# Attention and a gated feed-forward block: where eight blocks of probabilities are transposed

## The chip, the cores and the metric

The kernel runs on one core of a Trainium2 chip. The metric is the device time of one execution in microseconds (us). A core has five engines that run their own instruction lists in order and wait for each other by semaphores: TensorE (PE in the profile, with PEld for its weight loads), VectorE (DVE), ScalarE (ACT), GpSimd (POOL) and SyncE (SP), which here issues the DMA transfers.

## The reference

Sliding-window attention over 8 batches of 576 positions (8 heads of 64), whose output is the input of a gated feed-forward block on 4608 tokens.

```python
scores = scale * np.matmul(q, k.transpose(0, 1, 3, 2))
rel = pos[:, None] - pos[None, :]
mask = (rel >= 0) & (rel < window)          # window = 64
scores = np.where(mask, scores, -1000000000.0)
scores = scores - np.max(scores, axis=-1, keepdims=True)
attn = np.exp(scores)
attn = attn / (np.sum(attn, axis=-1, keepdims=True) + 1e-09)
out = np.matmul(attn, v)
...
x = np.ascontiguousarray(attn_out.transpose(0, 2, 1, 3)).reshape(B * S, H * D)
gate = 1.0 / (1.0 + np.exp(-(x @ w_gate)))
val = x @ w_val
return gate * val @ w_out
```

## The kernel before, in words

**Tiles and pairs.** The 4608 tokens are 12 tiles of 384; two tiles are a pair. The first pair goes through the feed-forward block by plain matrix products. The other five pairs (`s` = 1 to 5; the text calls `s` = 2 the second pair and `s` = 3 the third) use seven block products for each step of the 2 x 2 block scheme. Every number is held as a high and a low part, so that a product is three matmuls (line 641).

**Ups and downs.** The ups of a pair have 42 steps: 6 values of `k` by 7 products, and in each step one product for the gate half (`m` = 0) and one for the value half (`m` = 1), six matmuls each. Three PSUM banks per half are used again for all seven products; ScalarE copies the first product out (line 656), VectorE adds the others (lines 651 and 680), ScalarE makes the gate (`g`, line 424) and VectorE multiplies gate and value (`h<-g,...`, line 429). The downs have 42 steps as well, each with three matmuls for either output half (`y_0`, `y_1`), in the same six banks. Their right-hand sides are split parts of the hidden values: ScalarE writes the high part (line 723), VectorE the low one (line 724).

**Attention beside it.** A unit is one tile by one pair of heads. The attention of the pairs to come runs inside the ups, in visits. A visit (`stage_v`) at up 5, 12, 19, 26 or 33 forms the outputs of the last two units (line 380) and the scores of two new ones (line 225); VectorE adds the mask and takes the minimum (line 250), ScalarE the exponentials with their sums (line 258), VectorE inverts the sums (lines 265 and 266), GpSimd multiplies by them (line 275). Then the probabilities have to be transposed, half by half (two heads, two halves, `h`). There are two ways:

- `stage_b`: three matmuls with the identity on TensorE (line 329) and a copy by ScalarE (line 334) per half.
- `stage_d` and `stage_e`: ScalarE copies the 32-bit words into two planes of 16 bits (`pl`, line 347), a DMA transposes the planes (`plT`, line 350), and ScalarE joins them again (line 357).

In the visits of new units of the same next pair the first unit goes by planes and the second by TensorE. In the last visit of the second and third pair's ups, at up 33, the two units belong to the pair after the next, and both go by TensorE.

**What sets the order.** Every step is put on a list with a time of the plan's own clock, and the list is sorted; buffers rotate in the order of that list. A scheduler then lays each engine's instructions out in an order that keeps these dependences. The planes `pl` come from a ring of three buffers (`w32`), and so do `t1` tiles that prepare the next pair's input: `x_prep` forms, for either of two column blocks, the differences `t` and `xf` (lines 595 and 596). The transposed planes lie in buffers of the pool `xp` which the plan knows to be free. q and k of a unit have two buffers each (`q` and `k`), filled by loads on SP.

Of the kernel before, what the change touches and what calls it, by code (L numbers as in the profile page):

```python
# [14 lines left out]
U16 = mybir.dt.uint16  # L15
# [4 lines left out]
P = 128  # L20
# [3 lines left out]
UP = UT // 2  # L24
# [3 lines left out]
def attn_ffn(ctx: ExitStack, tc: tile.TileContext, qT, kT, vN, w_gate, w_val, w_out, out, outT):  # L28
# [9 lines left out]
    NP = DM // P  # L38
# [12 lines left out]
    xp = ctx.enter_context(tc.tile_pool(name="xp", bufs=1))  # L51
    mp = ctx.enter_context(tc.tile_pool(name="mp", bufs=2))
    ap = ctx.enter_context(tc.tile_pool(name="ap", bufs=1))
# [113 lines left out]
    xs, xf = {}, {}  # L167
# [169 lines left out]
                marks["pT"][NP * t + p] = cp.ins  # L337
            st[(t, p, h)] = pT

    def stage_d(t, p):  # L340


        free = [unit(t // 2, i) for i in (6, 7)]
        for h in range(2):
            halves = st[(t, p, h)].rearrange("p u c -> p (u c)").bitcast(U16).rearrange("p (n e) -> p e n", e=2)
            pl = mp.tile([P, 2, TT], U16, name=f"pl{h}_{t}_{p}", tag="w32", bufs=W32)
            nc.scalar.copy(pl, halves)
            ft, fp = free[h]
            plT = xp.tile([P, 2 * UP, P], U16, name=f"plT{h}_{t}_{p}", tag=f"xf{4 * (ft % 2) + fp}")
            nc.sync.dma_start_transpose(out=plT, in_=pl.rearrange("p e n -> p (e n)"))  # L350
            turned_of[(t, p, h)] = plT

# [410 lines left out]
    def put(tm, o, f, *a):  # L763
        events.append((tm, o, f, a))

    AHEAD = 2
    DPT = DNT / TB
    APT = (0.9, 0.8, 0.9, 1.5, 0, 2.7, 0, 0)
    stages = (stage_a, stage_b, stage_c, stage_s, stage_n, stage_v, stage_d, stage_e)
    LOAD_AHEAD = 8  # L770
    BEFORE, BEHIND = 0, 12
# [9 lines left out]
    for n in range(2 * NP):  # L781
        t, p = divmod(n, NP)
# [6 lines left out]
    def unit(s, n):  # L789
        return 2 * s + n // 2 % 2, n // 4 + n % 2 * 2  # L790
# [11 lines left out]
    for n, (x, y, z) in enumerate(((4.5, 7.5, 8.5), (9, 12, 13), (13.5, 16, 17), (17.5, 20.5, 22), (22.5, 25, 26), (26.5, 30, 31), (31.5, 35, 36), (36.5, 40, 41))):  # L802
        u = unit(1, n)
# [5 lines left out]
    def attend(i):  # L809
        nonlocal now  # L810
        for f, t, p, *done in fill.get(i, ()):
            if f == 5:
                for a in t or ():
                    put(now - LOAD_AHEAD, 8, load_qk, *a)
                    put(now + 2.8, 8.5, load_v, *a)
            if f in (0, 3):
                ahead = LOAD_AHEAD + (1.5 if t // 2 == 2 else 0)
                put(now - ahead, 8, load_qk, t, p)
                put(now - ahead, 8.5, load_v, t, p)
            put(now, 6, stages[f], t, p, *done)  # L820
            now += APT[f]
# [60 lines left out]
    for s in range(1, NS):  # L882
        fill.clear()

        def visit(key, *what):
            fill.setdefault(key, []).append(what)

        if s + 1 < NS:
            done = [unit(s + 1, i) for i in range(2)] if s > 2 else None
            for v, u in enumerate(DOUBLE):  # L890
                if s == 1 or done and v == 0:
                    continue
                new = [unit(s + 1, 2 * v + i) for i in range(2)] if v < NP else None
                if v == NP and s + 2 < NS:
                    new = [unit(s + 2, i) for i in range(2)]
                visit(("u", u), 5, new, done)
                for i, (a, tn, tb) in enumerate(zip(new[::-1] if new else (), (1.5, 2.5), (3.5, 5))):
                    visit(("u", u + tn), 4, *a)
                    if i == 0 and v < NP:
                        visit(("u", u + 2.5), 6, *a)  # L900
                        visit(("u", u + 6.5), 7, *a)
                    else:
                        visit(("u", u + tb), 1, *a)
                done = new
        if s == 1:
            visit(("u", 1), 1, *unit(s + 1, 0))
            for v, u in enumerate(VISITS, 1):
                visit(("u", u), 3, *unit(s + 1, v), unit(s + 1, v - 1), u % NPR)
                visit(("u", u + 1), 4, *unit(s + 1, v))
                visit(("u", u + 3.5), 1, *unit(s + 1, v))  # L910
            visit(("u", 41), 2, *unit(s + 1, 7))
        for k in range(NK):
            if s == 1:
                for m in range(2):
                    make = (-28 + 7 * m, -29 + 6 * m)[k] if k < 2 else -25 + 8 * m
                    put(now + make - 6, 7, sums_load, m, k)
                    put(now + make, 7, sums_make, m, k)
                    for i, at_cut in zip((0, 2), (-14 + 2 * m, -10 + 2 * m) if k == 0 else (-13 + 1.5 * m, -5 + 1.5 * m)):
                        put(now + at_cut, 7, sums_split, m, k, i)
                        put(now + at_cut + 4, 7, sums_store, m, k, i)  # L920
                for n, d in ((0, -23 if k == 0 else -14), (4, -12 if k == 0 else -4), (5, -9 if k == 0 else -1)):
                    put(now + d, 7.5, w_load, s, k, n)
            else:
                for n in range(NPR):
                    put(now - 22 + 2.1 * n, 7.5, w_load, s, k, n)
            for n in range(NPR):
                for m in range(2):
                    put(now, 9, product, s, k, n, m)
                    now += PRT
                    if m == 0:  # L930
                        attend(("u", NPR * k + n - 0.5))
                attend(("u", NPR * k + n))
            put(now + 0.5, 5, h_prep, s, k)
            if k < EXTRA:
                put(now + 3, 5.1, h_early, s, k)
        t0, at_down = now, []

        def x_parts(prep, free):
            for c in range(2):
                put(prep + 0.5 + c, 5, x_prep, s + 1, c)  # L940
                for n in range(NPR):
                    put(free(2 * n + c), 5.5, x_part, s + 1, n, c)
                    put(free(2 * n + c) + 0.9, 5.6, x_rest, s + 1, n, c)

        for n in range(NPR):
            if s == NS - 1 and n == NPR - 1:
                for q in range(2):
                    for k in range(NK):
                        if q == 0:
                            at_down.append(now)  # L950
                        put(now, 9, last_product, s, n, k, (q,))
                        now += PRT / 2
                continue
            for k in range(NK):
                at_down.append(now)
                put(now, 9, last_product, s, n, k)
                now += PRT
                attend(("d", NK * n + k))
        for i, tm in enumerate(at_down):
            if i < EXTRA + 2 * NPR:  # L960
                when = max(t0 - 14.5 + 2.1 * ((i - EXTRA) // 2 + 1), t0 - 5.2 if GUARD[0] <= i < GUARD[1] else t0 - 15, {5: t0 + 0.8, 11: t0 + 0.9, 17: t0 + 1}.get(i, t0 - 20))
            else:
                when = at_down[i - 19] + 1.2
            if i >= EXTRA:
                put(when, 5.2, h_part, s, *divmod(i, NK))
            if i % 2 == 0:
                put(at_down[i - 13] + 1.1 if i > 13 else t0 - 80 + 4 * i if s > 1 else t0 - 18 + 2 * i, 8.2, wo_load, s, i // 2)
        if s + 1 < NS:
            x_parts(at_down[20], lambda x: at_down[24 + x] + 1.3)
# [76 lines left out]
```

## Time and profile before

| | us |
|---|---|
| median of 3 runs | 940.41 |
| lowest, highest | 939.93, 940.72 |
| the profiled execution | 941.92 |
| span of its records | 940.1 |
| TensorE busy in the span | 924.1 |
| VectorE busy | 714.2 |
| ScalarE busy | 524.1 |

The granted clock of TensorE was full in every slice. A row in order of time gives its start, its length (from the first to the last end where it groups several), the engine, the line, the operation, the tiles and, in brackets, how long the engine was idle ahead of it and what ended that. Lengths overlap a little: on VectorE one 128x384 row is 0.55 us long, and the next starts 0.47 us after it.

### The profile page before, as it was taken

The numbers are of one execution on the slowest core, as the hardware profiler recorded it, in microseconds if no ns is written. First come the engines' busy times: TensorE is split into PE (matmuls) and PEld (weight loads), VectorE is DVE, ScalarE is ACT, GpSimd is POOL, SyncE is SP. The second block draws the span as 40 slices with busy tenths as digits, with TensorE's granted clock in tenths as the row PEclk, the third lists the DMA queues.
The fourth block names the chain that finished last, engine by engine and source line by source line (L and its number), as shares of the span: only waits on it lengthen the run. The fifth ranks groups of instructions, "written<-read, shape, count | busy, mean of one in ns | idle before, by whom it ended". The sixth has DMA issues, their size and how long they took to land.

```text
span 940.1 us, 20226 instructions
## 1 busy us (share of the span) xinstructions
PE 924.1 (98%) x7104; PEld 889.5 (95%) x7104; DVE 714.2 (76%) x1919; ACT 524.1 (56%) x1394; POOL 152.4 (16%) x232
## 2 busy tenths in 40 slices
PE   6999999999999999999999999999999999999998
PEld 4799999879999999999999999999999999999998
DVE  7999989788878975666985667796566896566882
ACT  7867677556566642766753276664156665222460
POOL 4211104703773000221100012100011100000000
PEclk9999999999999999999999999999999999999999
DMA  9899988979999989999889899989899788988475
GB/s 339 309 391 374 353 312 284 342 283 353 396 322 303 409 295 307 302 312 305 275 254 312 263 309 319 291 245 281 294 299 309 224 249 276 290 256 252 134 216 166
DMA packets 121510, 277.39 MB, mean 295 GB/s; under 512 B 27456, under 2 KB 49600, under 8 KB 121408
## 3 DMA queue, kind: packets, MB, share of 16 engines
q1 hardware_dynamic: 121408, 276.09, 89.1%
q8 instruction: 57, 0.93, 0.4%
q14 instruction: 45, 0.37, 0.1%
HBM read 220.20 MB, written 51.90 MB: 289 GB/s over the span
## 4 chain that ended last, share of the span: by engine, by line
PE 88%; DVE 5%; DMA 3%; ACT 2%; issue 1%; SPq 0%; POOL 0%; DVEq 0%; ACTq 0%; POOLq 0%
PE pr L641 45%; PE y L641 23%; PE ph L416 7%; PE y L464 3%; PE pr L380 2%; PE pp L329 2%; PE s L225 1%; ACT p L258 1%; DVE p L250 1%; PE pr L225 1%; PE s L380 1%; DMA a<-w32d 1%; DVE w L160 1%; DMA plT<-pl 1%; DMA q<-in_qT_dram 1%
## 5 line engine op out<-in xcount | busy, mean ns | idle before, releaser
L641 PE MATMUL pr<-x_T,wt 128*128 128x384 f32 x1224 | 221.7, 334 | 0.0
L641 PE MATMUL y<-h,wot 128*128 128x384 f32 x1260 | 219.9, 334 | 0.0
L641 PEld LDWEIGHTS y<-h,wot 128*128 128x128 f32 x1260 | 218.3, 188 | 0.7 <-DVE h L429 0.6
L641 PEld LDWEIGHTS pr<-x_T,wt 128*128 128x128 f32 x1224 | 212.8, 188 | 0.3 <-issue 0.3
L641 PE MATMUL pr<-x_B,wt 128*128 128x384 f32 x1008 | 188.4, 337 | 0.0
L641 PEld LDWEIGHTS pr<-x_B,wt 128*128 128x128 f32 x1008 | 174.4, 188 | 2.4 <-issue 1.9
L275 POOL TENSOR_TENSOR p<-p,rs 128x384 f32<-128x384 f32 x76 | 70.6, 942 | 515.6 <-DVE rs L266 240.0
L723 ACT CAST h<-h 128x384 fp32r<-128x384 f32 x210 | 104.3, 514 | 86.7 <-PE y L641 41.0
L724 DVE TENSOR_TENSOR h<-h,h 128x384 fp32r<-128x384 f32 x210 | 112.0, 562 | 23.2 <-ACT h L723 21.3
L258 ACT ACTIVATE p<-p,mn 128x128 f32<-128x128 f32 x288 | 110.9, 393 | 18.0 <-DVE mn L250 17.5
L416 PE MATMUL ph<-x,w 128*128 128x384 f32 x576 | 106.0, 338 | 0.9 <-DVE h L429 0.8
L416 PEld LDWEIGHTS ph<-x,w 128*128 128x128 f32 x576 | 99.7, 188 | 3.7 <-DVE h L429 1.3
L424 ACT ACTIVATE g<-c 128x384 f32<-128x384 f32 x90 | 47.0, 522 | 86.3 <-DVE c L680 80.1
L651 DVE TENSOR_TENSOR c<-pr,p 128x384 f32<-128x384 f32 x60 | 33.1, 551 | 36.3 <-PE pr L641 36.2
L429 DVE SCALAR_TENSOR_TENSOR h<-g,c 128x384 f32<-128x384 f32 x90 | 52.5, 583 | 8.0 <-ACT g L424 2.3
L258 ACT ACTIVATION_READ_ACCUMULATOR p<-p,mn 128x1 f32 x264 | 49.9, 189 | 0.0
L656 ACT COPY p<-pr 128x384 f32<-128x384 f32 x60 | 28.3, 474 | 36.6 <-PE pr L641 36.5
L651 DVE TENSOR_TENSOR u<-pr,p 128x384 f32<-128x384 f32 x60 | 33.0, 552 | 17.3 <-PE pr L641 17.3
L357 ACT COPY p<-plT 128x768 uint16<-128x768 uint16 x20 | 18.5, 926 | 40.7 <-DMA plT<-pl 40.7
L641 PE MATMUL pr<-x_T,ws 128*128 128x384 f32 x216 | 40.5, 339 | 0.0
L641 PEld LDWEIGHTS pr<-x_T,ws 128*128 128x128 f32 x216 | 37.2, 188 | 0.9 <-issue 0.3
L680 DVE TENSOR_TENSOR c<-pr,p 128x384 f32<-128x384 f32 x60 | 32.8, 554 | 5.3 <-PE pr L641 5.1
(188 smaller groups left out, 1246.2 us busy)
## 6 DMA issues: line engine op xcount, KB each, us to landing
wt<-wd SPq DMA_DIRECT2D x186, 512.0 KB, 4.6
wot<-wod SPq DMA_DIRECT2D x105, 512.0 KB, 4.7
v<-in_vN_dram SPq DMA_DIRECT2D x48, 384.0 KB, 5.7
wd<-ws SPq DMA_DIRECT2D x48, 256.0 KB, 5.5
k<-in_kT_dram SPq DMA_DIRECT2D x48, 224.0 KB, 5.6
q<-in_qT_dram SPq DMA_DIRECT2D x48, 192.0 KB, 5.6
w32d<-w SPq DMA_DIRECT2D x36, 256.0 KB, 5.1
wd<-w SPq DMA_DIRECT2D x36, 256.0 KB, 5.5
```

The lines of the kernel that those rows point to most:

```text
L258: exp = nc.scalar.activation(pt[:, u, :], pt[:, u, :], AF.Exp, bias=mn[:, u:u + 1], scale=-1.0, **sums)
L275: eng.tensor_mul(out=pt, in0=pt, in1=rs.unsqueeze(2).broadcast_to([P, UP, P]))
L380: pe(nc.tensor.matmul(oo[U // 2][h * BLK:(h + 1) * BLK, U % 2 * BLK:(U % 2 + 1) * BLK], vt[:, U, h * BLK:(h + 1) * BLK], pT[h][:, U // 2, ...
L416: pe(nc.tensor.matmul(ph, l, r, start=i == 0, stop=i == len(prs) - 1))
L424: act = nc.scalar.activation(g, c, AF.Tanh)
L429: nc.vector.scalar_tensor_tensor(out=out, in0=g, scalar=1.0, in1=val, op0=ALU.add, op1=ALU.mult)
L641: pe(nc.tensor.matmul(ps, l, r, start=first and i == 0, stop=last and i == 2, skip_group_check=not check))
L651: marks["plus"] = nc.vector.tensor_add(out=o, in0=ps, in1=a).ins
L656: nc.scalar.copy(st["p1"], ps)
L680: nc.vector.tensor_add(out=c, in0=in0, in1=in1)
L723: nc.scalar.copy(h2[:, 0, :], src)
L724: nc.vector.tensor_sub(out=h2[:, 1, :], in0=src, in1=h2[:, 0, :].bitcast(F32))
```

## The change

In the last visit of the second and third pair's ups both units go by planes. The planes of one unit are transposed into the two `q` buffers, those of the other into the two `k` buffers; the joins are put on the list at downs 3 and 5.

```diff
-    def stage_d(t, p):
-
-
-        free = [unit(t // 2, i) for i in (6, 7)]
+    def stage_d(t, p, last):
+
+
         for h in range(2):
...
             nc.scalar.copy(pl, halves)
-            ft, fp = free[h]
-            plT = xp.tile([P, 2 * UP, P], U16, name=f"plT{h}_{t}_{p}", tag=f"xf{4 * (ft % 2) + fp}")
+            if last:
+                plT = ap.tile([P, 2 * UP, P], U16, name=f"plT{h}_{t}_{p}", tag=last, bufs=2)
+            else:
+                ft, fp = unit(t // 2, 6 + h)
+                plT = xp.tile([P, 2 * UP, P], U16, name=f"plT{h}_{t}_{p}", tag=f"xf{4 * (ft % 2) + fp}")
             nc.sync.dma_start_transpose(out=plT, in_=pl.rearrange("p e n -> p (e n)"))
...
                     visit(("u", u + tn), 4, *a)
-                    if i == 0 and v < NP:
-                        visit(("u", u + 2.5), 6, *a)
-                        visit(("u", u + 6.5), 7, *a)
+                    if i == 0 or v == NP:
+                        visit(("u", u + (2.5, 5)[i]), 6, *a, "qk"[i] if v == NP else None)
+                        visit(("u", u + 6.5) if v < NP else ("d", (3, 5)[i]), 7, *a)
                     else:
                         visit(("u", u + tb), 1, *a)
```

The order of the instructions moves at three places, in the second pair and in the same way in the third. The first is VectorE in the last visit of the ups. Before, one of the two preparing differences (`t_3_1`) and its partner (`xf_1`) stand among the masked minima (`ISA`), the other two rows (`t_3_0`, `xf_0`) some twenty rows earlier.

```order
L250 ISA p_8_2_6528,mn_8_2_6529<-pr_0_2_4_6336,m_81 128x128
L250 ISA mn_8_2_6529 128x1
L595 TENSOR_TENSOR t_3_1_7032<-xf_1_6524,xf_1_6245 128x384
L250 ISA p_8_2_6537,mn_8_2_6538<-pr_1_2_4_6365,m_81 128x128
L250 ISA mn_8_2_6538 128x1
L250 ISA p_8_2_6537,mn_8_2_6538<-pr_1_2_4_6327,m_81 128x128
L250 ISA mn_8_2_6538 128x1
L596 TENSOR_TENSOR xf_1_6524<-xf_3_6526,xf_1_6524 128x384
L250 ISA p_8_2_6528,mn_8_2_6529<-s_(8, 0)_6498,m_81 128x128
```

In the change the minima stand there without them. The second place is VectorE some forty rows on, at the end of the ups. Of the change, from the split part ahead of the first difference to the gate product that reads `pr_1`'s first bank:

```order
L726 TENSOR_TENSOR h_2_3_6714<-h_2_3_6141,h_2_3_6714 128x384
L597 TENSOR_TENSOR t_3_0_7018<-xf_0_5964,xf_0_5679 128x384
L597 TENSOR_TENSOR t_3_1_7032<-xf_1_6524,xf_1_6245 128x384
L726 TENSOR_TENSOR h_2_4_6717<-h_2_4_6422,h_2_4_6717 128x384
L682 TENSOR_TENSOR c_1_2_5_6683<-pr_1_2_5_6656,c_1_2_5_6681 128x384
...
L598 TENSOR_TENSOR xf_0_5964<-xf_2_5966,xf_0_5964 128x384
L682 TENSOR_TENSOR c_0_2_5_6729<-pr_0_2_5_6609,p_0_2_5_6592 128x384
L598 TENSOR_TENSOR xf_1_6524<-xf_3_6526,xf_1_6524 128x384
L607 TENSOR_TENSOR h_2_4_6422<-h_2_4_6423,h_2_4_6422 128x384
L431 SCALAR_TENSOR_TENSOR h_2_5_6686<-g_11_6673,c_1_2_5_6683 128x384
L431 SCALAR_TENSOR_TENSOR h_2_5_6685<-g_5_6702,pr_1_2_5_6600 128x384
```

All four preparing rows now stand ahead of that gate product; From the row of line 265 that takes up the last unit's sums (`rs_0`) to that gate product it is 25 rows before and 29 now. The third place is ScalarE at the end of the ups. Before, the two gates of the last product (`g_11`, `g_5`) stand beside two copies out of PSUM:

```order
L723 CAST h_2_0_6724<-h_0_5342 128x384
L424 ACTIVATE g_11_6675<-c_0_2_5_6673 128x384
L334 COPY p_8_0_6545<-pp_8_0_6690 128x384
L334 COPY p_8_0_6554<-pp_8_0_6695 128x384
L424 ACTIVATE g_5_6706<-pr_0_2_5_6585 128x384
L723 CAST h_2_1_6737<-h_1_5577 128x384
```

And now, from the last of the four plane copies:

```order
L346 COPY pl_8_0_6692<-p_8_0_6554 128x768
L359 COPY p_8_2_6528<-plT_8_2_6627 128x768
L725 CAST h_2_4_6717<-h_2_4_6422 128x384
L725 CAST h_2_0_6720<-h_0_5342 128x384
L359 COPY p_8_2_6537<-plT_8_2_6631 128x768
L426 ACTIVATE g_11_6673<-c_0_2_5_6671 128x384
L359 COPY p_8_0_6545<-plT_8_0_6690 128x768
L426 ACTIVATE g_5_6702<-pr_0_2_5_6585 128x384
L725 CAST h_2_1_6733<-h_1_5577 128x384
L725 CAST h_2_2_6736<-h_2_2_5862 128x384
L359 COPY p_8_0_6554<-plT_8_0_6694 128x768
```

Three joins stand ahead of the gate `g_5`, the fourth three rows behind it, all of them still in the ups' part of ScalarE's list. On SP the four transposes stand among the weight loads of the next pair, and the loads of the next q and k behind the fourth of them.

## Rows read from the trace of the kernel before

**Rows 1.** The page, part 1: busy time, share of the span and instructions of the engines that compute.

```profile
PE 924.1 (98%) x7104; PEld 889.5 (95%) x7104; DVE 714.2 (76%) x1919; ACT 524.1 (56%) x1394; POOL 152.4 (16%) x232
```

**Rows 2.** Busy time by stretch: the stretch, its length, then the busy us (and instructions) of PE, PEld, DVE, ACT and POOL, the granted clock, the DMA share and GB/s. The end of the second and third pair's ups, then the start of their downs.

```profile
449.00:468.00 19.00, 19.00 (x137) 18.76 (x130) 17.38 (x58) 13.58 (x46) 3.66 (x4) 1.00 0.83 274
597.00:616.00 19.00, 19.00 (x136) 18.76 (x129) 17.48 (x57) 13.49 (x45) 3.67 (x4) 1.00 0.82 267
468.00:484.00 16.00, 16.00 (x94) 15.96 (x93) 15.47 (x33) 10.88 (x23) 0.00 (x0) 1.00 0.84 257
616.00:632.00 16.00, 16.00 (x94) 16.00 (x93) 15.28 (x33) 10.69 (x23) 0.00 (x0) 1.00 0.86 253
```

**Rows 3.** The chain that ended last, in order of time: start, length, what. The four groups of transposes that the change takes away, and the downs of the two pairs.

```profile
457.21 0.66 PE pp L329 x6
...
460.99 0.65 PE pp L329 x6
...
467.89 43.70 PE y L641 x252
...
605.19 0.65 PE pp L329 x6
...
608.99 0.66 PE pp L329 x6
...
615.89 43.68 PE y L641 x252
```

**Rows 4.** TensorE in order of time at the change from ups to downs of the second pair.

```profile
465.65 2.24 PE L641 MATMUL pr<-x_B,wt 128*128 128x384 f32 x12
467.73 22.54 PE L641 MATMUL y<-h,wot 128*128 128x384 f32 x129
```

**Rows 5.** VectorE in order of time, from the last visit of the second pair's ups into its downs.

```profile
449.12 0.29 DVE L250 CUSTOM_DVE_ANT_0 p<-pr,m 128x128 f32<-128x128 f32 x1
...
449.55 0.56 DVE L595 TENSOR_TENSOR t<-xf,xf 128x384 f32<-128x384 f32 x1
...
450.44 0.56 DVE L596 TENSOR_TENSOR xf<-xf,xf 128x384 f32<-128x384 f32 x1
...
455.24 0.36 DVE L265 SCALAR_TENSOR_TENSOR rs<-rs 128x6 f32<-128x6 f32 x1 [1.45 <-ACT p L258]
...
457.28 1.18 DVE L724 TENSOR_TENSOR h<-h,h 128x384 fp32r<-128x384 f32 x1
...
462.24 0.55 DVE L651 TENSOR_TENSOR c<-pr,p 128x384 f32<-128x384 f32 x1
...
467.38 0.55 DVE L429 SCALAR_TENSOR_TENSOR h<-g,pr 128x384 f32<-128x384 f32 x1
...
476.74 3.37 DVE L724 TENSOR_TENSOR h<-h,h 128x384 fp32r<-128x384 f32 x7
```

**Rows 6.** VectorE in order of time in the visit before that one, at up 26.

```profile
430.57 0.29 DVE L250 CUSTOM_DVE_ANT_0 p<-pr,m 128x128 f32<-128x128 f32 x1 [0.79 <-ACT xf L312]
...
435.75 0.35 DVE L265 SCALAR_TENSOR_TENSOR rs<-rs 128x6 f32<-128x6 f32 x1 [1.45 <-ACT p L258]
...
436.25 0.53 DVE L595 TENSOR_TENSOR t<-xf,xf 128x384 f32<-128x384 f32 x1
...
438.28 0.71 DVE L596 TENSOR_TENSOR xf<-xf,xf 128x384 f32<-128x384 f32 x1
...
446.19 0.56 DVE L429 SCALAR_TENSOR_TENSOR h<-g,pr 128x384 f32<-128x384 f32 x1 [2.55 <-ACT g L424]
```

**Rows 7.** ScalarE in order of time: the first plane copy of the visit at up 26, and the gate of the last visit's stretch that reads the first bank.

```profile
436.40 0.83 ACT L347 COPY pl<-p 128x768 uint16<-128x768 uint16 x1
...
463.52 0.50 ACT L424 ACTIVATE g<-pr 128x384 f32<-128x384 f32 x1
```

**Rows 8.** SP's queue in order of time in the visit at up 26 (the two transposes), then all joins (shortest, median and longest in ns), and the time from the issue of a transpose to its landing.

```profile
437.26 1.23 SPq L350 DMA_TRANSPOSE plT<-pl  x1
...
439.20 1.22 SPq L350 DMA_TRANSPOSE plT<-pl  x1
...
L357 ACT COPY p<-plT x20: 921/926/935, 385.9 to 739.9; 128x768 uint16<-128x768 uint16 x20
...
DMA to landing us min/median/max: 3.4/4.5/6.0
```

## The prediction

> **What bounds the kernel now.** I read the busy shares first, then the chain of work that ended last, then the busy time by stretch, and last VectorE's and ScalarE's rows in order of time at the place that the change touches. The shares [rows 1] show TensorE at 98% of the span and VectorE at 76%. Taken alone they say that an instruction taken off TensorE is worth its length. The chain [rows 3] agrees so far: the four visits whose transposes go stand on it with 0.66, 0.65, 0.65 and 0.66 us.
>
> The stretch table is what changes the picture [rows 2]. From 449 to 468 us, the end of the second pair's ups, VectorE is busy 17.38 of 19.00 us, and from 468 to 484, the start of its downs, 15.47 of 16.00. The third pair is much the same at 597 to 632. Here two engines are full at once. In order of time [rows 5] VectorE's last idle stretch is the one ahead of 455.24, where it waits for an exponential of ScalarE; from there no row has idle time until after 480 us. TensorE's downs begin at 467.73 [rows 4]; 252 matmuls in 43.70 us [rows 3] are 0.1734 us each, so they run without a gap. How close VectorE is behind decides everything, and there are two places where it is close:
>
> - Place A. The second output half's first matmul writes the bank that `h<-g,pr` (line 429) reads. That row runs 467.38 to 467.93; the matmul comes three matmuls after 467.73, at 468.25. 0.32 us are spare.
> - Place B. The last split part of the second product of the downs is the fifth row of the group of seven at 476.74: it starts at 478.62 and ends at 479.17. It is read by the 68th matmul of the downs, 67 x 0.1734 after 467.73, at 479.35. 0.18 us are spare.
>
> So at both places TensorE could come hardly any earlier than it does, whatever is taken off it.
>
> **The change part by part.** The times below are those of the profiled execution (span 940.1, itself 941.92 us; the median of the three runs is 940.41, 1.5 less). I work out a difference and put it on the median. I follow the second pair; the third is the same program 148 us later.
>
> *Transposes on TensorE.* 2 units x 6 transposes a pair go, 0.65 + 0.66 = 1.31 us [rows 3]. If nothing else held TensorE, the downs would begin at 467.73 - 1.31 = 466.42 and place A would be reached at 466.94.
>
> *VectorE's rows.* The four preparing rows of the next pair's input (`t`, `xf`; lines 595, 596) get their buffer from the ring that the new planes use. The planes come ahead of them in that ring, so, as the order shows, they move behind the planes: from places at 436.25, 438.28, 449.55 and 450.44 [rows 5, 6] into the full stretch, ahead of `h<-g,pr`. Two effects follow.
> First a gain. Two of the rows stood inside the masked minima that feed the exponentials. From the first minimum to the row that waits for the last exponential it is 455.24 - 449.12 = 6.12 us here and 435.75 - 430.57 = 5.18 in the visit before, which has none of them inside [rows 5, 6]. So VectorE's full stretch begins 0.94 earlier, at 454.30. (The other two stood ahead of an idle 2.55 us at 446.19 [rows 6]; taking them away there gains nothing.)
> Then the loss. From 455.24 to `h<-g,pr` at 467.38 it is 12.14 us for 25 rows, with GpSimd's slowing in it. The changed order has the same 25 and the four more; a row is followed by the next after 0.47, so 1.88. Without any wait `h<-g,pr` starts at 454.30 + 12.14 + 1.88 = 468.32. I add 0.05, since the sum `u` cannot start before TensorE's product, which isn't earlier: 468.37.
>
> *The transposes by DMA.* The first plane copy follows VectorE's waiting row by 436.40 - 435.75 = 0.65 us and its transpose by 437.26 - 435.75 = 1.51; the second was issued 1.94 later, with a weight load between [rows 5 to 8]. So I expect issues at 455.8, 457.75 and, with SP's 1.22 us per transpose and no load between, the third at about 459.05. The median landing is 4.5 us, from 3.4 to 6.0 [rows 8]. Input preparation needs two of them, since each `t` overwrites a plane: the second lands at 462.25, before its `t` at 462.75, and the third at 463.55, after its own at 463.22 (both counted from 462.24 [rows 5], less 0.89, with the rows between). The wait is 0.33; at 3.4 us it is nothing, at 6.0 it is 1.8. Behind it on VectorE stand all rows up to `h<-g,pr`, and TensorE waits for them. I take the median: `h<-g,pr` from 468.70 to 469.25.
>
> The Trainium skill, DMA: Bandwidth & Descriptors, Latency and other measured facts, gives a DMA transpose an effective 261 GB/s, which for one plane of 196,608 bytes would be an estimate of 0.75 us. By it the third would be there soon after its issue, the wait would be nothing, and the sum some 2.5 us; the row's 3.4 us at the least from issue to landing says otherwise here.
>
> *Place A:* 469.27 instead of 468.25 for the second half's first matmul, a loss of 1.0 us, though TensorE was there at 466.94. *Place B:* in the changed order the row is the 25th behind `h<-g,pr` instead of the 24th: 468.70 + 25 x 0.468 = 480.40 to 480.95. TensorE, late by 1.0, would read it at 480.37. Another 0.6 us. Behind that the split parts are ahead of it. Per pair 1.6, for two pairs 3.2 us: 941.92 + 3.2 = 945.1 in that execution's terms, 943.6 on the median.
>
> *ScalarE.* Four plane copies and four joins (0.93 us each [rows 8]) replace four copies. The diff puts the joins into the downs by its own clock, but the order has all four ahead of, or just behind, the two gates at the end of the ups, so ScalarE waits for landings there. The gate that frees the first bank runs at 463.52 now [rows 7]. In the change it stands behind the third join: 463.55 + 0.93 + 0.5 = 465.0, still ahead of 466.42. So this is free by 1.4 us; a landing at 6.0 would use that up, but VectorE's wait on the same transfer is then longer. *SP.* Loads of q and k move behind the joins, and weight loads behind transposes by some 2 to 4 us; the weights are those of the next pair's ups, 44 us later, and q and k of its second visit. I take nothing; what would show it is TensorE waiting for a load at 512 us.
>
> **The rivals.**
>
> *Late landings.* If the third transpose takes 6.0 us, the wait is 1.8 instead of 0.33, each pair 3.1, and the time 940.41 + 6.2 = 946.6. For it: the weight loads share the queue. Against it: q and k loads leave this stretch, and DMA is at 0.83 here [rows 2].
>
> *Out of GpSimd's way, no change.* The 12.14 us contain a row of 1.18 us in place of 0.55, at 457.28, while GpSimd multiplies [rows 5]. If the shifted rows miss that and the third transpose is in time, place A costs 1.0 - 0.33 - 0.63 = 0.04 and only place B's 0.6 is left: 0.64 a pair, 941.7. Against it: GpSimd follows the same exponentials, so it shifts by the same 0.94. The Trainium skill, SBUF — State Buffer, SBUF: two separate sides, has VectorE with two SBUF inputs and GpSimd exclude each other for a whole instruction; the row at 457.28 fits that, and by it the collision comes again.
>
> *TensorE's share decides, faster.* The whole 2.6 us comes through: 937.8. It needs `h<-g,pr` done by 466.94, and the split part by 478.04. For it: 98% against 76%, and TensorE on the chain throughout. Against it: even now the row ends at 467.93, and of its 1.0 us the earlier start gives 0.94 only if the four rows cost nothing.
>
> **How the numbers follow.** Forecast 943.6, chance 0.58, with its own range 942.4 to 945.2 (landings of 3.4 to 5.3 us). Late landings 0.12. No change 0.22. Faster 0.08. What a measurement can tell from no change is 0.2%, 1.9 us. That gives slower 0.70, same 0.22, faster 0.08. The range 940.0 to 946.0 holds the forecast, most of the unchanged case and the near side of late landings.
>
> **What would show it.** Right: the row that waits for the exponential about 0.9 us earlier; no idle on VectorE behind it but for a short one at the second `t` that a transpose ends; TensorE idle some 2.3 us at the second matmul group of the downs with VectorE's `h<-g,pr` as releaser, and again shortly at the 68th matmul; downs that take 46 instead of 43.7 us. The page's transposes fall from 228 to 204. Wrong: downs that begin at 466.4 and run without a gap, or TensorE waiting for a load of the next pair's ups.

## The result, and the profile after

The changed kernel takes 945.44 us (median of 6 runs, 944.52 to 948.51) against 940.18 for the kernel before on the same chip: a ratio of 1.0061, 95% interval 1.0047 to 1.0076. It is slower by 5.3 us where 3.2 were forecast. The two profiled executions are 948.51 (the slowest of its six) and 941.92 us, so between the two traces 6.6 us have to be found. All times here are those of executions in the fast state; one of the twelve of run e1, 1682.64 us at a granted clock of 0.82, is left out.

The page, part 1, answers to [rows 1]: TensorE has the 24 transposes fewer, and is busy no shorter for it: for a stretch its clock was lower, as told below.

```profile
PE 927.3 (98%) x7080; PEld 891.4 (94%) x7080; DVE 713.2 (75%) x1919; ACT 532.6 (56%) x1402; POOL 152.8 (16%) x232
```

The chain that ended last, in order of time, at the start of the second pair's downs (start, length, what). Before, these downs were one piece of 252 matmuls [rows 3].

```profile
467.78 0.94 DVE h L431 x2
...
468.77 8.62 PE y L643 x39
...
477.40 0.52 ACT h L725
...
479.45 2.36 DVE h L726 x5
...
481.85 32.36 PE y L643 x185
```

TensorE goes on twice because VectorE lets it: at 468.77, after the row `h<-g,pr` (place A of the prediction), and at 481.85, after the last split part of the second product (place B, the 68th matmul). TensorE in order of time (in brackets the idle time ahead of a row, and what ended it) answers to [rows 4]:

```profile
464.07 2.24 PE L643 MATMUL pr<-x_B,wt 128*128 128x384 f32 x12
466.15 0.68 PE L643 MATMUL y<-h,wot 128*128 128x384 f32 x3
468.77 17.53 PE L643 MATMUL y<-h,wot 128*128 128x384 f32 x88 [1.94 <-DVE h L431]
```

VectorE in order of time, the same stretch, answers to [rows 5]:

```profile
454.14 0.36 DVE L265 SCALAR_TENSOR_TENSOR rs<-rs 128x6 f32<-128x6 f32 x1 [1.45 <-ACT p L258]
...
456.65 0.71 DVE L598 TENSOR_TENSOR h<-h,h 128x384 f32<-128x384 f32 x1
...
462.31 1.26 DVE L597 TENSOR_TENSOR t<-xf,xf 128x384 f32<-128x384 f32 x2
...
468.16 0.55 DVE L431 SCALAR_TENSOR_TENSOR h<-g,pr 128x384 f32<-128x384 f32 x1
...
477.29 1.22 DVE L726 TENSOR_TENSOR h<-h,h 128x384 fp32r<-128x384 f32 x2 [1.09 <-ACT h L725]
...
613.80 1.18 DVE L597 TENSOR_TENSOR t<-xf,xf 128x384 f32<-128x384 f32 x2 [0.63 <-issue]
```

The last line is the third pair's. The two `t` rows overwrite planes, and each has to wait until the transpose that reads its plane has landed. I call this the landing wait: how much later than four steps of 0.47 us (1.88) the row behind the two `t` starts, counted from the start of the two split parts ahead of them. In this profile it is 0.45 us in the second pair (463.48 - 461.15 - 1.88) and 0.86 in the third (614.89 - 612.15 - 1.88). The profile names a transpose as what ends it in two runs only (e3 and e6); for the others it is inferred from the buffer, and from e2, which has no planes there and no such wait.

And busy time by stretch around the idle (columns as in [rows 2]; the number before the DMA share is the granted clock):

```profile
466.00:468.70 2.70, 0.83 (x5) 0.51 (x3) 2.70 (x7) 2.18 (x5) 0.00 (x0) 1.00 1.04 390
468.70:470.00 1.30, 1.23 (x6) 1.24 (x7) 1.30 (x4) 0.92 (x2) 0.00 (x0) 0.83 1.09 425
470.00:472.00 2.00, 2.00 (x8) 2.00 (x7) 2.00 (x6) 0.62 (x2) 0.00 (x0) 0.50 0.98 377
472.00:474.00 2.00, 2.00 (x11) 2.00 (x10) 2.00 (x5) 0.76 (x2) 0.00 (x0) 0.76 0.73 252
```

The fall of the clock was not forecast. TensorE is busy 0.83 of 2.70 us, and behind that its granted clock falls to 0.50, 1.2 in place of 2.4 GHz. The 39 matmuls from 468.77 take 8.62 us; at 0.1734 each they would take 6.76. The buffers they read come free later, ScalarE casts later (`h`, line 725), and VectorE has 1.09 us of idle at 477.29 and is later at place B.

**A measure for one pair.** From the last output products of the last visit's stretch (the 48 short matmuls of line 380, in the changed kernel 382) to the end of the downs, all that the change moves in the pair's own order is inside. It is read from the chain (start, length, what; the downs end where the next pair's products begin). The kernel before, in its second profile (e9):

```profile
447.37 1.55 PE pr L380 x48
...
512.43 7.63 PE pr L641 x44
```

The changed kernel, in its first:

```profile
446.42 1.55 PE pr L382 x48
...
514.21 5.89 PE pr L643 x34
```

So 65.06 us before and 67.79 changed: 2.7 more. I call this the stretch of a pair and use it for all runs:

| kernel | median us | stretch, second pair | third pair |
|---|---|---|---|
| before, two profiles | 940.2 to 940.6 | 65.01, 65.06 | 65.37, 65.21 |
| changed, first profile | 945.44 | 67.79 | 67.99 |
| changed, second profile (e5) | 945.39 | 66.29 | 66.18 |
| e1, e8: changed, rows held past both places | 938.90, 939.54 | 63.92, 63.91 | 63.92, 63.93 |
| e11: changed, rows in another ring | 938.79 | 63.93 | 63.92 |
| e2: before, rows late | 944.96 | 66.73 | 66.73 |
| e3: changed, transposes done twice | 942.57 | 67.11 | 66.93 |
| e4: before, rows held | 940.45 | 65.37 | 65.02 |
| e6: changed, idle filled | 944.17 | 67.12 | 66.49 |
| e7, e10: changed, rows between the places | 947.57, 944.96 | 66.40, 66.40 | 66.38, 66.40 |

### The profile page after: what moved, and what is told of

The parts are those of the page before. It is cut to its first block, busy times and chain, and to the rows that moved or that the text cites. A ratio compares the mean times of both kernels' runs of the same rounds, so it can differ in the third digit from the quotient of the medians.

```text
span 946.7 us, 20200 instructions
## 1 busy us (share of the span) xinstructions
PE 927.3 (98%) x7080; PEld 891.4 (94%) x7080; DVE 713.2 (75%) x1919; ACT 532.6 (56%) x1402; POOL 152.8 (16%) x232
## 4 chain that ended last, share of the span: by engine, by line
PE 82%; DMA 6%; DVE 5%; ACT 4%; issue 1%; SPq 1%; POOL 0%; DVEq 0%; ACTq 0%; POOLq 0%
PE pr L643 40%; PE y L643 23%; PE ph L418 8%; PE y L466 3%; DMA plT<-pl 2%; PE pr L382 2%; ACT p L258 2%; PE pp L329 2%; PE s L225 1%; DMA raw<-in_moe_w_val_dram 1%; DVE h L726 1%; PE pr L225 1%; PE s L382 1%; DMA w32d<-w 1%; ACT pl L346 1%
## 5 line engine op out<-in xcount | busy, mean ns | idle before, releaser
L643 PE MATMUL y<-h,wot 128*128 128x384 f32 x1260 | 223.9, 338 | 4.5 <-DVE h L431 4.2
L643 PEld LDWEIGHTS y<-h,wot 128*128 128x128 f32 x1260 | 221.1, 190 | 6.5 <-DVE h L431 5.5
L653 DVE TENSOR_TENSOR c<-pr,p 128x384 f32<-128x384 f32 x60 | 33.1, 551 | 39.1 <-PE pr L643 39.1
L359 ACT COPY p<-plT 128x768 uint16<-128x768 uint16 x28 | 25.9, 925 | 44.9 <-DMA plT<-pl 44.9
L431 DVE SCALAR_TENSOR_TENSOR h<-g,pr 128x384 f32<-128x384 f32 x30 | 16.6, 552 | 27.8 <-ACT g L426 24.6
```

The lines of the kernel that those rows point to most:

```text
L431: nc.vector.scalar_tensor_tensor(out=out, in0=g, scalar=1.0, in1=val, op0=ALU.add, op1=ALU.mult)
L643: pe(nc.tensor.matmul(ps, l, r, start=first and i == 0, stop=last and i == 2, skip_group_check=not check))
L653: marks["plus"] = nc.vector.tensor_add(out=o, in0=ps, in1=a).ins
```

## The experiments

The theory: the four preparing rows (`t`, `xf`), pushed by the planes' ring into VectorE's full stretch, make TensorE wait at places A and B. The rivals: the landings, joins and plane copies do it; or TensorE's own work still decides. None of these kernels changes the output.

**e1 and e8, the rows out of the way.** The edit to the changed kernel; it holds the fifth pair's rows as well, which the texts on record don't say:

```diff
-        with tc.issue_after(marks["plus"]) if s == 2 else nullcontext():
+        with tc.issue_after(marks["plus"]) if s > 1 else nullcontext():
             differences(nc.vector, b11, b12, b22, t1)
```

> The changed kernel, with the four preparing rows (t, xf) of the third and fourth pair's input held back until the downs before have added their first sums, so that they are out of VectorE's full stretch ahead of the last output splits. Nothing else is changed; the output is the same. Theory (the four rows push the row h<-g,pr, and TensorE waits for it): without them that row ends near 467.0 us in place of 468.71, TensorE reaches the second half's first matmul without an idle of more than 0.3 us, the granted clock stays 1.0 there, and the saving of 1.3 us a pair comes through: 937.5 to 938.5 us, below both kernels. Rival (the landings of the planes or the joins hold the end of the ups): the idle of about 2 us stays, and so does the time, 944.5 to 946. Rival (VectorE is full without the four rows as well): half of the idle stays, 940 to 942.

Measured: 938.90 us, a little above what was expected, ratio to before 0.9988 (0.9979 to 0.9997). VectorE and TensorE in order of time:

```profile
453.21 0.35 DVE L265 SCALAR_TENSOR_TENSOR rs<-rs 128x6 f32<-128x6 f32 x1 [1.45 <-ACT p L258]
...
464.89 0.55 DVE L682 TENSOR_TENSOR c<-pr,p 128x384 f32<-128x384 f32 x1
465.36 0.54 DVE L431 SCALAR_TENSOR_TENSOR h<-g,pr 128x384 f32<-128x384 f32 x1
...
474.34 3.36 DVE L726 TENSOR_TENSOR h<-h,h 128x384 fp32r<-128x384 f32 x7
```

```profile
463.12 2.24 PE L643 MATMUL pr<-x_B,wt 128*128 128x384 f32 x12
465.20 20.97 PE L643 MATMUL y<-h,wot 128*128 128x384 f32 x118
```

From the row that takes up the sums to the end of `h<-g,pr` it is 12.69 us here (465.90 - 453.21) and 14.57 in the changed kernel (468.71 - 454.14): 1.88 apart. That this is four times 0.47 is chance: in e1 a further sum (`c`, at 464.89) stands ahead of `h<-g,pr`, so only three rows are fewer, 1.41, and the rest is the landing wait of 0.45, which goes with the `t` rows. The idle is gone, with planes, joins and transposes by DMA all still there: what these cost at this place, they cost by way of the four rows, which they push back and keep waiting. A pair gains 1.1 us of the 1.31: at place A TensorE would be there 0.52 after 465.20, at 465.72, and the row ends at 465.90. That the whole is 1.6 and not 2.2 us shorter is told under the fourth pair below. Again, beside the changed kernel:

> The kernel of e1 once more, beside the changed kernel on the same chip: whether it is faster than the kernel before by more than the measurement is uncertain, and by how much it is below the changed kernel. Theory: 938 to 939.3 us, 6 to 7 us below the changed kernel, no idle of TensorE over 0.3 us at the start of the downs. Rival (the gain in e1 was chance): 940 to 941.

939.54 us, ratio 0.9989 (0.9981 to 0.9998), 5.9 below the changed kernel measured beside it (e5): just short of the 6 to 7 expected, and a gain of only a tenth of a per cent over before.

**e4, the same hold in the kernel before** (the same line).

> The kernel before with the four preparing rows held back in the same way as in the run of the changed kernel (e1): VectorE is relieved, TensorE keeps its transposes. The output is the same. Theory (TensorE bounds the kernel before at that place, VectorE is 0.2 to 0.3 us ahead): no change, 939.5 to 940.8 us; so what the run e1 gains comes from TensorE's transposes and not from the rows' new place. Rival (the rows' place alone is worth something, by clock or by a hidden wait): 938 to 939.3 us.

940.45 us, ratio 0.9998 (0.9989 to 1.0007), as expected. Relief for VectorE alone is worth nothing; e1's gain is TensorE's 1.31 us, let through.

**e2, the rows alone.** The kernel before, transposes on TensorE, the rows behind a split part late in the ups:

```diff
-        with tc.issue_after(marks["plus"]) if s == 2 else nullcontext():
+        with tc.issue_after(marks["plus"] if s == 2 else marks["hs", s - 1, 1, 3]) if s in (2, 3, 4) else nullcontext():
...
-        nc.vector.tensor_sub(out=h2[:, 1, :], in0=src, in1=h2[:, 0, :].bitcast(F32))
+        marks["lo"] = nc.vector.tensor_sub(out=h2[:, 1, :], in0=src, in1=h2[:, 0, :].bitcast(F32)).ins
...
+        marks["hs", s, n, k] = marks["lo"]
```

> The kernel before, all transposes of the last visit left on TensorE, with only the four preparing rows of the third and fourth pair's input moved to where the changed kernel has them (behind a split part late in the ups). The output is the same. Theory (the moved rows alone make the loss at the start of the downs): h<-g,pr ends 0.5 to 1.0 us later, TensorE waits 0.3 to 0.7 us for it at the second half's first matmul and again at the split part of the second product, some 1.1 us a pair, no drop of the granted clock since the idle is short: 942 to 943 us. Rival (the planes, joins and transposes by DMA make it, not the rows): no change from before, 939.9 to 940.6.

944.96 us, ratio 1.0044 (1.0032 to 1.0056): the loss without the new planes. VectorE, then TensorE:

```profile
453.98 0.35 DVE L265 SCALAR_TENSOR_TENSOR rs<-rs 128x6 f32<-128x6 f32 x1 [1.45 <-ACT p L258]
...
456.01 1.18 DVE L724 TENSOR_TENSOR h<-h,h 128x384 fp32r<-128x384 f32 x1
...
468.94 0.54 DVE L429 SCALAR_TENSOR_TENSOR h<-g,pr 128x384 f32<-128x384 f32 x1
```

```profile
467.34 0.69 PE L641 MATMUL y<-h,wot 128*128 128x384 f32 x3
469.54 16.75 PE L641 MATMUL y<-h,wot 128*128 128x384 f32 x95 [1.51 <-DVE h L429]
```

It is more than the 1.1 us a pair expected: 14.96 us from the sums to `h<-g,pr` against 12.14 before is 2.82, six rows and not four. The scheduler put two further rows, a split part and a sum, ahead of it. So the run shows that late rows alone make such a loss, without any landing, and not how much of it is the four.

**e3, TensorE's work put back.** The changed kernel with the 24 transposes done on TensorE as well, unread, and the rows pinned as in e2:

```diff
+    def stage_x(t, p):
+        for h in range(2):
+            pt = st[(t, p, h)]
+            pp = bank(t, p, f"p{h}", f"pp{h}_{t}_{p}")
+            for u in range(UP):
+                pe(nc.tensor.transpose(pp[:, u, :], pt[:, u, :], ident))
...
+                        if v == NP:
+                            visit(("u", u + tb), 8, *a)
```

> The changed kernel with the 24 transposes of the last visits done on TensorE a second time, with nobody reading them, and the preparing rows pinned to where the changed kernel has them: 12 instructions a pair more on TensorE, 1.3 us, all other engines as in the changed kernel. The output is the same. Theory (VectorE's row sets when the second half's first matmul can go, and the idle ahead of it is what the granted clock falls after): the release comes at the same time, TensorE's idle ahead of it shrinks from about 2 to about 1 us, the granted clock falls less or not at all, and the time is not longer than the changed kernel's: 942.5 to 945.5 us. Rival (TensorE's own work still counts at that place): 2.6 us longer than the changed kernel, 947.5 to 948.5.

942.57 us, ratio 1.0023 (1.0013 to 1.0033): 1.3 us of work more on TensorE in either pair, and the time is lower, not 2.6 higher: the rival falls. TensorE's idle ahead of place A is shorter, and the clock keeps its 2.4 GHz (the last line, by stretch):

```profile
467.64 0.69 PE L650 MATMUL y<-h,wot 128*128 128x384 f32 x3
469.51 11.37 PE L650 MATMUL y<-h,wot 128*128 128x384 f32 x64 [1.18 <-DVE h L438]
```

```profile
470.00:472.00 2.00, 2.00 (x13) 2.00 (x12) 2.00 (x5) 1.03 (x2) 0.00 (x0) 1.00 1.06 409
```

By how much it is lower (2.9 us) the trace doesn't explain: the profiled execution, 944.37, is the slowest of the seven, and its pairs lose 2.1 and 1.7, 0.8 more than in e5. Most of that is the landing wait, 0.92 and 0.86 us here against 0.33 and 0.23 there; 0.1 to 0.2 us a pair are left that TensorE's added work may cost.

**e5, the changed kernel again.**

> The changed kernel once more, unaltered, beside the runs below on the same chip: its spread, and a second profile. If the granted clock at the start of the downs falls in this execution too (to 0.5 behind an idle of 2 us), it belongs to the change and not to one execution: 944.5 to 946 us, with the idle at the second half's first matmul at 1.9 to 2.3 us in both pairs. If the clock stays at 1.0 in this profile, the idle alone has to make the loss, and the time is at the low end, 944 to 944.8.

945.39 us, ratio 1.0059 (1.0044 to 1.0073); the profiled execution 945.22. VectorE, TensorE, and one stretch:

```profile
454.90 0.36 DVE L265 SCALAR_TENSOR_TENSOR rs<-rs 128x6 f32<-128x6 f32 x1 [1.45 <-ACT p L258]
...
461.91 1.02 DVE L726 TENSOR_TENSOR h<-h,h 128x384 fp32r<-128x384 f32 x2
462.97 1.24 DVE L597 TENSOR_TENSOR t<-xf,xf 128x384 f32<-128x384 f32 x2
464.12 0.55 DVE L726 TENSOR_TENSOR h<-h,h 128x384 fp32r<-128x384 f32 x1
...
468.80 0.54 DVE L431 SCALAR_TENSOR_TENSOR h<-g,pr 128x384 f32<-128x384 f32 x1
...
478.63 3.36 DVE L726 TENSOR_TENSOR h<-h,h 128x384 fp32r<-128x384 f32 x7
```

```profile
467.08 0.68 PE L643 MATMUL y<-h,wot 128*128 128x384 f32 x3
469.40 11.39 PE L643 MATMUL y<-h,wot 128*128 128x384 f32 x64 [1.64 <-DVE h L431]
481.11 9.13 PE L643 MATMUL y<-h,wot 128*128 128x384 f32 x51 [0.32 <-DVE h L726]
```

```profile
470.00:472.00 2.00, 2.00 (x14) 2.00 (x13) 2.00 (x5) 1.03 (x2) 0.00 (x0) 1.00 1.04 405
```

The clock stays here, behind an idle of 1.64 us in place of 1.94, and a pair loses 1.0 to 1.2 us, not 2.7. So a fall of the clock belongs to some executions of the changed kernel only; what it costs in them is worked out in the next section. But the expectation that a kept clock brings the time to 944 to 944.8 is a miss: 945.22.

**e6, the idle filled.** TensorE repeats the first three matmuls of the downs three times, starting the sum over:

```diff
+            for _ in range(3 if s in (2, 3) and (n, k, q) == (0, 0, 0) else 0):
+                three(st[b][:, :TT], wot[(s, n, k)], q, hs[(s, n, k)], True, False, False)
             three(st[b][:, :TT], wot[(s, n, k)], q, hs[(s, n, k)], n < 3 and k == 0, k == NK - 1, n < 3)
```

> The changed kernel, in which TensorE computes the first output half's first group of the downs (3 matmuls) three times more in the second and third pair, each time starting the sum over, so that 1.56 us of its idle ahead of the second half's first matmul are filled with work that changes no result; every other engine's order is as in the changed kernel. Theory A (the loss is idle plus a granted clock that falls after it): the clock stays 1.0, the casts of ScalarE behind the downs' first matmuls are not held up, VectorE has no idle of 1.1 us ahead of the second split, and each pair is 0.6 to 1.0 us shorter: 943 to 944.2 us. Theory B (only VectorE's rows decide when TensorE goes on, the clock costs nothing): no change from the changed kernel, within 0.5 us. Theory C (matmuls of TensorE cost wherever they stand): 3.1 us longer.

944.17 us, ratio 1.0046 (1.0028 to 1.0063). Theory C falls: 3.1 us of matmuls don't make it longer. The median is 1.2 us below that of the changed kernel, where theory A put it, but the two intervals overlap. In the trace TensorE's idle ahead of place A is down to 0.81 and 0.47 us and the clock stays at 1.00, and yet the stretches of the two pairs are 0.83 and 0.31 us longer than in e5, where the idle wasn't filled and the clock held too. VectorE shows why:

```profile
460.19 1.02 DVE L726 TENSOR_TENSOR h<-h,h 128x384 fp32r<-128x384 f32 x2
461.99 0.56 DVE L597 TENSOR_TENSOR t<-xf,xf 128x384 f32<-128x384 f32 x1 [0.78 <-issue]
462.76 0.56 DVE L597 TENSOR_TENSOR t<-xf,xf 128x384 f32<-128x384 f32 x1 [0.21 <-DMA plT<-pl]
463.24 0.55 DVE L726 TENSOR_TENSOR h<-h,h 128x384 fp32r<-128x384 f32 x1
```

The landing wait is 1.17 us here (463.24 - 460.19 - 1.88) against 0.33 in e5, and 0.56 against 0.23 in the third pair; these differences, 0.84 and 0.33, are those of the stretches. So next to an execution in which the clock holds, filling the idle is worth nothing, as theory B has it. What a fall of the clock costs, these two traces can't show.

**e7 and e10, the rows between the places.** The rows wait for `h<-g,pr`; in e7 for `s > 1`, in e10 for the two pairs alone:

```diff
-                gated(hidden(s, k)[2 * r + b], c, gates.pop((t, j)))
+                done = gated(hidden(s, k)[2 * r + b], c, gates.pop((t, j)))
+                if (n, k) == (4, NK - 1):
+                    marks["A"] = done
...
-        with tc.issue_after(marks["plus"]) if s == 2 else nullcontext():
+        with tc.issue_after(marks["plus"] if s == 2 else marks["A"]) if s in (2, 3, 4) else nullcontext():
```

> The changed kernel with the four preparing rows of the third and fourth pair's input held only until the row h<-g,pr, so that they are behind place A (the second half's first matmul) and still ahead of place B (the last split part of the downs' second product). The output is the same. Theory (both places bind, each by itself): TensorE has no idle over 0.3 us at place A and one of some 1.6 us at place B, released by VectorE's split, so each pair loses 1.6 of the 1.1 it gains: 941 to 942.5 us. Rival (only place A counts): 938.5 to 939.5, as with the rows held past both places (e1). Rival (A's loss merely moves and the clock falls as in the changed kernel): 944 or more.

> As e7, with the rows held until h<-g,pr in the third and fourth pair's input alone; those of the fifth stand where the changed kernel has them (in e7 they were held as well, and the fourth pair's downs paid for it). The output is the same. Theory (what the four rows cost does not depend on whether they stand ahead of place A or between A and B, since VectorE is full up to B): no idle at place A, idle time in pieces up to the 68th matmul that sums to 2.4 to 2.7 us a pair, and the time of the changed kernel: 944 to 945.8 us. Rival (place A is dearer than place B): 941 to 943.

e7 took 947.57 us (ratio 1.0084, 1.0071 to 1.0096), a miss in two ways: the edit reached the fifth pair's input too, and the fourth pair's downs, which had no such loss, then paid it as well (a stretch 2.5 us longer than in e10); and a pair comes out 1.2 to 1.3 us longer than before, not 0.5. e10 took 944.96 us (1.0053, 1.0040 to 1.0066), as expected. TensorE in e10:

```profile
466.75 5.90 PE L643 MATMUL y<-h,wot 128*128 128x384 f32 x31
473.12 6.35 PE L643 MATMUL y<-h,wot 128*128 128x384 f32 x35 [0.46 <-DVE h L728]
479.86 0.44 PE L643 MATMUL y<-h,wot 128*128 128x384 f32 x1 [0.39 <-ACT h L727]
481.09 9.11 PE L643 MATMUL y<-h,wot 128*128 128x384 f32 x51 [0.79 <-DVE h L728]
```

Place A is passed without a wait, and the 68th matmul comes at 481.09 all the same: 14.34 us after the downs' first instead of 67 x 0.1734 = 11.62, so 2.7 us are lost in pieces, where e5 loses 481.11 - 467.08 - 11.62 = 2.4 in two. What binds is VectorE's sum of rows up to place B.

**e9, the kernel before again.**

> The kernel before, unaltered, for a second profile: 939.5 to 941 us. The stretches from the last visit's first value product to the end of the downs should read as in the first profile, 65.0 us in the second pair and 64.9 to 65.0 in the third, without idle time of TensorE at the start of the downs. What the two profiles of the same kernel differ by elsewhere (the stages ahead of 318 us, and the visits of the second to fourth pair that wait for a transpose by DMA) is what no theory of the change has to explain; if that is 1 us or more, the loss of 5 us in the medians holds a part that a comparison of two single profiles can't show.

940.64 us, as expected; the profiled execution 942.42, the slowest of its ten. TensorE has no idle at the start of the downs. The stretches by the measure above are in the table; the run serves the account below.

**e11, another ring.** The differences `t` get their buffers from the ring `raw`, nothing is written about their order:

```diff
-        t1 = mp.tile([P, TT], F32, name=f"t1_{s}_{c}", tag="w32", bufs=W32)
+        t1 = mp.tile([P, TT], F32, name=f"t1_{s}_{c}", tag="raw" if s > 2 else "w32", bufs=RAW if s > 2 else W32)
```

> The changed kernel with the two buffers of the preparing rows (the differences t) of the third to fifth pair's input in the ring of six that the raw weights use, in place of the ring of three that the planes use. No order is written for the rows; the output is the same. Theory (it is the shared ring that puts the rows into VectorE's full stretch, and where they go instead, behind the split parts, costs nothing): as with the rows held (e1, e8), 938.3 to 939.8 us, no idle of TensorE over 0.3 us at the start of the downs. Rival (the rows' lateness costs on the other side, in the splits of the later products or the next pair's input): 940.5 or more.

938.79 us, ratio 0.9990 (0.9981 to 0.9999). TensorE runs through the change to the downs:

```profile
464.86 2.24 PE L643 MATMUL pr<-x_B,wt 128*128 128x384 f32 x12
466.94 23.32 PE L643 MATMUL y<-h,wot 128*128 128x384 f32 x132
```

It is the ring shared with the planes that put the rows where they hurt. With this ring the four stand at 484.15 to 486.51, behind the split part that place B waits for, where they cost nothing. The first of them:

```profile
484.15 0.56 DVE L597 TENSOR_TENSOR t<-xf,xf 128x384 f32<-128x384 f32 x1
```

## Why the prediction was right, and where its sizes were off

**Right: the mechanism.** Two engines full at once, the rows pushed by the ring, a wait at place A and again at B. e2 shows a loss from late rows alone (six of them), e1, e8 and e11 its end when the four go. Point by point, with e5 shifted by 0.60 us so that its 48 output products (447.18) begin where those of the first profile of before do (446.58):

- *TensorE, 1.31 us less a pair.* Right; e1 brings 1.1 of it out.
- *Gain of 0.94 ahead of the row that takes up the sums.* Forecast 454.30; e5 454.90 - 0.60 = 454.30.
- *Four rows, 1.88.* Right by count: from the sums to `h<-g,pr` it is 29 rows in e5 and 25 before, each followed by the next after 0.47.
- *Wait for the landing at the second `t`, 0.33.* e5: 464.12 - 461.91 - 1.88 = 0.33 in the second pair, 0.23 in the third. Right in its place, but the exact hit is luck: the first profile has 0.45 and 0.86, e3 0.92 and 0.86, e6 1.17 and 0.56. So the rival "late landings" came true in part, in some executions. Over all transposes of the first profile, the time from issue to landing answers to [rows 8]:

```profile
DMA to landing us min/median/max: 3.1/4.6/6.9
```

  The estimate of 0.75 us from the Trainium skill (DMA: Bandwidth & Descriptors, Latency and other measured facts) is far below the least of them, so the trace's bound was the one to take.
- *`h<-g,pr` at 468.70.* e5: 468.20. This is the first step that failed: the 12.14 us were taken over with GpSimd's slow row of 1.18 in them [rows 5]. In the changed kernel no row there is longer than 0.72, 0.46 us less. This was the rival "out of GpSimd's way", and it came true for this part: 12.14 + 1.88 + 0.33 - 0.46 = 13.89, and e5 has 468.80 - 454.90 = 13.90. The sentence that by the Trainium skill (SBUF — State Buffer, SBUF: two separate sides) the collision would come again held only in small part: in e5 two rows beside GpSimd's take 0.64 and 0.70 us in place of 0.55. e2, with the old order at that place, has the row of 1.18 again.
- *25 rows from there to place B, 11.70.* e5: from the row's end, 469.34, to the end of the fifth split part, 478.63 + 4 x 0.47 + 0.55 = 481.06, 11.72. Right.
- *1.6 us a pair.* With 0.46 off, 1.14; e5 measures 1.2 and 1.0 by the stretch. A slip in the forecast's own range: at landings of 3.4 us the wait of 0.33 goes, a pair loses 1.27, and the range should have begun at about 943 and not at 942.4.
- *ScalarE and SP, nothing.* No trace has TensorE waiting for a gate at the end of the ups, or for a load when the next pair begins. For the visits of the fourth pair it can't be said (below).

**Missing: the clock.** I counted the idle of 2.3 us at its length. In the first profile, behind 1.94 us in the second pair and 2.31 in the third, the clock fell to 0.50, and place B came 13.1 and 12.9 us behind the end of `h<-g,pr` instead of 11.7: some 1.4 and 1.2 us more. The stretches of these pairs are 1.50 and 1.81 us longer than in e5; the rest is the longer landing wait, 0.12 and 0.63 us. In e5 the clock didn't fall.

**The fourth pair, open.** From the end of the third pair's downs to the start of the fourth's it is 101.82, 101.33, 101.62 and 100.99 us in the kernels with the old transposes (before twice, e2, e4), and 102.68, 102.32, 101.80, 102.84, 102.16, 102.83 and 102.46 with the new (changed twice, e6, e10, e1, e8, e11): 1.0 more on average. The place is a visit of the fourth pair's ups, with the same instructions in the same order as before, whose second join waits for its transpose (`plT`): 0.24 us in both profiles of before, 2.09 and 2.96 in those of the changed kernel. ScalarE's gate behind it comes later, and TensorE is idle for it 1.12 and 0.93 us, against 0.47 at the most in the kernels with the old transposes. e3, with the new transposes, waits 0.64 there, has no such idle and 100.91 us, and speaks against a simple rule. What in the queue makes these landings later wasn't tried.

**The account.** Between the profiles of e5 and e9 (945.22 and 942.42, 2.8 apart) it is 1.2 and 1.0 in the two pairs and 1.0 in the fourth, less 0.4 elsewhere. Between the first two (6.6 apart) it is 2.8 and 2.6 in the pairs, 0.9 in the fourth and 0.3 elsewhere. In the medians the loss is 4.9 to 5.3 us, between the two: the forecast of 3.2 was two pairs at 1.6, against some 1.1 or 2.7 for each as the clock and the landings go, with the fourth pair's 1.0 not foreseen. That the forecast came this near is in part luck: 0.5 us a pair too much stood against the fourth pair and the clock, which it didn't have. How often the clock falls can't be read off the executions without a trace. Both profiled executions of before lie 1.5 us and more above its median; why is open. So it is luck, too, that 945.1, the sum in that execution's own terms, lies nearer to the result than the 943.6 put on the median.

## What to carry to other kernels

Where two engines are full at once, work taken off the one comes through only if the other doesn't get later: follow the wait that ends last on both sides before counting the gain. A new buffer taken from a shared ring moves whoever takes the next one, on another engine, past it; look for these rows in the new order first, and give them another ring or another place (here that turned 5 us of loss into 1 to 1.6 us of gain). Place them behind the last wait and not merely behind the first: between two waits they cost the same (e10). A row that overwrites what a transfer still reads waits for that transfer as well, and this wait differs from one execution to the next (here by up to 0.9 us).

## What the hardware showed that was not expected

An idle of TensorE can cost more than its length. Behind idles of 1.94 and 2.31 us (one execution) the granted clock fell to 0.50, 1.2 in place of 2.4 GHz; over the next 2 us it was 0.76 and 0.71 on average, and then full again. Ahead of these idles, from 460 to 466 us and from 611 to 617, TensorE had been busy all the time. Behind 1.10 and 1.18, 1.51 and 1.56, and 1.64 and 1.71 us (e3, e2 and e5, each in its two pairs) it stayed at 1.00. No run varied the idle alone, so this is what these executions show and no more. TensorE was back at work, and it was ScalarE's casts and VectorE's splits that were made later by its slow matmuls.
